# Second layernorm's statistics in two operations instead of three for the later twelve token tiles, with a new order of all operations up to the mix's first tile pair

## The chip, the cores and the metric

The kernel runs on one core of a Trainium2 chip. The metric is device time in microseconds (us) from start to end of one execution, the median of several runs. A core has five engines that each work through their own queue of instructions in order: PE (TensorE, matrix products; PEld is its loading of weights), DVE (VectorE), ACT (ScalarE), POOL (GpSimd) and SP (SyncE, which here only issues DMAs). An instruction waits at the head of its queue until what it reads is there; everything behind it on that engine waits too.

## The reference, cut to what matters

```
x = A_q                                              # [1, 2048, 640], bf16
sa, ca, ga, sb, cb, gb = split((silu(c) @ w_mod), 6)
h = layernorm(x) * (1 + ca) + sa                     # first layernorm
kv = shift_conv(A_k, 4 taps) * A_v                   # short convolution along the tokens
y  = irfft(rfft(kv, 4096) * rfft(ssm_k, 4096))[:2048] + kv * ssm_D   # long convolution
x = x + ga * (h * y)
h = layernorm(x) * (1 + cb) + sb                     # second layernorm: mean and variance over 640 channels
z = gelu(h @ w_in)                                   # 640 -> 1728, tanh form
z1, z2 = z[..., :864], layernorm(z[..., 864:])
g = w_sp @ z2 + b_sp                                 # mix over the 2048 tokens
x = x + gb * ((z1 * g) @ w_out)                      # 864 -> 640
```

## The kernel before, in words

The 2048 tokens are 16 tiles n of 128 (partitions), four groups g of `TB = 4` tiles. The 640 channels are five units u of 128.

The first half works unit by unit. For each unit, PE makes the short convolution with diagonal weights (`dg`); DVE multiplies it with v (L570) and SP transposes the product with DMAs ("kx", L582). The long convolution is a two-step transform. "s1" (stage 1) and its copies to SBUF go first, for the taps ("K") and the signal ("U"). Then come eight steps st: PE's forward ("fwd") of K and U, a copy of the K side by ACT (L247, `KH`), the product by DVE (L463, `Tf`), two sums of its parts by POOL or DVE ("csum", L477, `W`) and PE's inverse ("inv", into `pz`), copied to `Z`. At the end of a unit Z is turned (a DMA, "zt", for units 0 to 3; PE's transposes, "zfl" with copies "zk", for unit 4, whose copies the prediction calls zc), PE makes the last stage y, and DVE multiplies it onto `gh` (L701 "ym", unit 4: L769 "yml"). `gh` holds the first layernorm's output: "ln1" takes its statistics (DVE: L603 and L604; ACT: L599 and L600), "xn" normalizes, and "ghm" (L684, POOL or DVE) multiplies by (1+ca)ga and adds sa ga. "res" (L721) adds `gh` to x (`xt`), and "ln2" (L727) takes the second layernorm's statistics of as many units as are done:

```
            if u not in (1, 3, 4):
                return
            us = range(u - (u < 4), u + 1)
```

So each tile n has three bn_stats: of units 0 and 1 (256 elements), of units 2 and 3 (256), of unit 4 (128). A bn_aggr ("ag2", L852) joins them, then rstd (POOL, L189 and L190, "rstd2"), nmr2 (DVE, L856) and the normalization "zx" (L866 on ACT, L868 on POOL, L870 on DVE). Token group 0 is done in two pieces of two tiles each, so that it gets on sooner; its output is transposed on PE ("hfl", L881) and modulated ("hmod", L892 on ACT, L894 on DVE). Groups 1 to 3 are turned by a DMA ("turn", L912) and modulated by "hmod2".

Then PE makes `zz`, the product with w_in (five matmuls of 432 columns each), ACT the gelu (L943), DVE the statistics of z2 (L949), and DVE or ACT its normalization ("zn", L964). Last is the mix with w_sp over pairs of token tiles (L1036, 48 matmuls of 432 columns for one product group) and the projection with w_out (L1160).

All operations up to the mix's first pair of tiles are not issued where the code stands. Each is recorded in `Plan` with what it reads and writes and with the engines that it may run on; `Plan.run` issues them by `ORDER`, a text written out by hand: a letter for the engine (P, A, D, G for POOL, S) and the number of the operation in the order of recording. So each engine's queue is the letters of its kind, in that order. Waits follow from data and buffers.

Numbers used below, the same in both orders: D36 is the last of the first unit's multiplications with v, S37 and S38 the two DMA transposes of its output, S524 to S527 the loads of the four quarters of x (L589), D532 the ln1 of tile 4, P186 the first forward of unit 0's signal, D187 the first product, P358 the inverse of step 4 of unit 2, G356 and G357 its two sums, G347 a sum of a step before, G446, G447 and G437 sums of unit 3. "gelut" (A133) is a gelu of one small tile that brings ACT's gelu table in. In the order before it stands behind the first gelus. Six "fill" operations are matmuls of the identity (128x512 each; 4, 6, 2, 2, 4 and 3 of them) that nobody reads. In the order before, the fill P1037 (four matmuls) stands between two transposes of unit 4.

Of the kernel before, what the change touches and what calls it, by code (L numbers as in the profile page):

```python
# [31 lines left out]
TB = 4  # L32
# [5 lines left out]


ORDER = """  # L40
A4 A1 S89 D0 G102 P1036 P1035 P7 D13 D15 S2 S90 D14 A16 D101 A10 D103 D116 D117 P1033 S23 G5 D6 A28 A118 D17 D104 D105
P8 A11 D92 A119 D91 A106 D110 D111 A107 P1034 D18 D20 S26 P146 A113 S25 D122 D123 A147 A148 P149 A151 A150 G27 P29 D30
A112 G114 D19 A124 P31 D32 P155 A156 P152 D153 S24 P33 D34 P35 D36 S93 A157 G108 G109 A154 D94 P158 A21 D22 S524 P134
A125 P228 D229 A115 G120 D128 A159 A135 D528 P164 A165 P162 A163 G121 P168 A169 P166 A167 S525 D532 P234 A235 G126
D529 G127 P172 A173 P170 A171 P137 S37 P174 P177 S38 D176 A175 D179 D138 G139 P1038 P140 D141 P183 A178 D184 S39 A530
G41 P180 D181 G42 G136 D531 P230 G54 G142 A182 A185 P186 D187 G188 S40 A231 P202 S52 D203 P232 A533 P43 G189 P45 G53
D44 S3 D46 A233 A534 A535 S527 P196 D197 G198 G199 P248 A249 P47 D48 P49 P190 P9 A12 P160 A161 P212 D50 S51 D536 G537
A191 P200 D213 G214 A543 G215 A201 P222 P55 D223 G224 G225 S566 D56 P218 P204 P192 D219 D193 P59 D538 G554 G555 D60
A544 A129 P252 A253 P206 D207 G131 G132 P143 D144 A205 D556 P236 A237 P254 A255 S526 P57 P194 P258 P242 G145 S95 A545
P250 D58 D259 A243 A251 P567 D539 A568 P569 D540 D541 A195 G67 P256 A257 P61 G550 G551 P220 A546 D96 P260 P302 A221  # L50
A303 P216 G552 D553 S571 G208 G209 D130 D261 P238 A239 P226 A217 A570 P292 P304 P240 A241 D542 D293 P210 P574 P246 D62
G79 A305 D547 S64 A227 D575 G262 G263 A247 P286 D287 A211 P308 A309 P572 P296 G557 D66 D710 D297 G548 D549 P264 P294
A295 D573 P306 A307 P244 P276 P68 A245 S63 P326 D613 D277 D298 P314 P266 A558 D265 P72 D267 A315 A327 P324 A325 G652
D592 G288 G289 P290 A291 P328 A329 G594 P310 A311 S65 D69 A562 P280 D73 D281 G299 P300 P74 D75 P270 A301 P330 A331
P322 S576 P577 A323 G559 G560 A561 P278 A279 D271 D272 D578 D595 D593 P316 D78 P332 A333 G282 G283 D650 A317 D617 S97
S77 D273 P579 D654 D98 P284 P70 D596 D597 P350 D618 A563 A564 D580 G651 S600 P376 A377 A285 D351 P274 A275 P80 D565
G598 D71 G599 P344 D345 G346 G347 P378 P334 A379 D335 G336 G337 D81 P268 A269 P312 A313 P380 A381 P601 D602 P320 A321
P366 D367 P82 P382 A383 D83 P370 D371 P603 P318 D604 S76 D615 P338 A319 G671 P400 A401 G614 P348 A349 D339 P388 A389
P605 P360 P402 A403 P352 A353 G372 D373 D606 P607 G619 G620 D361 G362 P354 D355 P404 A405 P340 D341 P368 D653 P386
A387 D616 P374 A375 P406 D672 A407 P384 A385 P398 S99 G363 A399 P84 D100 D356 G357 D675 P450 A451 D712 D708 G709 A369  # L60
D608 G609 P408 D409 D85 P390 A391 P86 D87 P454 A455 P414 S621 P622 D623 P364 P396 A397 A365 G673 D415 P452 P624 S88
D625 G410 P342 A453 A343 G411 P418 P358 A359 P392 A393 S581 P626 D656 G657 P456 D419 P428 D627 P440 D429 D441 P628
D629 G655 A457 D635 D610 P412 A413 G420 G421 P474 A475 D630 D634 P416 A417 P464 P394 A465 P422 A423 P480 A395 G430
A481 P444 D445 P442 A443 P424 G431 P432 D636 G446 G447 D425 D638 P476 P434 A477 A433 P582 A583 P458 G612 P478 D435
G436 G437 G677 G678 A479 S658 P659 D660 A459 D639 D633 P426 A427 P661 D662 P472 A473 P482 D483 P448 P438 A439 P663
D664 P466 A467 P498 P665 D499 A449 P518 S584 S679 D519 S757 G484 D666 P585 P462 G485 A463 P486 D711 G676 A586 G520
P460 A461 G645 A487 P502 D503 P488 D489 P500 D637 P468 A469 A501 P508 P492 P490 G504 D505 G521 A491 D509 P522 A523
G674 G714 D493 P470 P680 D681 P514 A471 D515 P506 A507 P682 G510 G511 P512 P516 D683 D632 P684 D649 D685 G494 G495
A513 A517 P496 A497 G670 D631 P686 D687 P720 G667 D688 D689 P716 P718 A721 P722 D717 A719 D723 P724 P726 P725 D690
D692 P727 D728 D729 D730 D731 G693 P736 G668 S587 S758 P588 D759 D760 G761 D694 P750 P1037 D732 D733 A589 D691 D762  # L70
A763 P590 A591 D764 D734 D737 D772 D735 D773 P765 D767 D768 D769 D738 G774 D739 P766 A770 A771 D697 G713 D696 D775
A777 D695 D740 D836 P743 P785 A786 D742 D838 P788 A789 P817 A818 D835 G776 P779 D741 D837 A783 D715 D751 D752 P813
D756 A814 G839 D840 D841 A784 P778 D780 D782 P792 A844 D843 G842 A793 P815 A816 D744 P819 S845 A820 P795 A796 D753
D781 P806 D745 D749 P799 A800 A807 D669 D698 D700 G640 G611 D642 P802 A803 D755 D643 P809 D703 A133 S1046 G849 S1045
A846 D644 P823 D747 D707 A810 D704 P825 A826 D702 D904 D706 A848 P821 P827 D641 D701 A822 A828 G847 G850 P851 A852
D748 D699 D790 D746 D901 D903 P858 D902 G905 S1039 D794 P872 D906 D648 A824 D801 D1047 P868 A907 A873 G910 P881 A869
D909 D908 S911 G916 D646 D797 A882 D798 D1054 D1053 D967 A859 P885 A886 D705 P875 P854 D754 S1041 P883 D970 A876 D787
D791 D647 A884 D860 D968 G914 P865 S1040 D870 A855 A866 D867 P861 D969 A862 G971 A915 P889 A890 P891 A892 D1049 A912
P887 A888 P879 D811 A880 D808 D812 D804 D805 G913 P893 D863 D864 A894 D856 D972 D973 D975 G829 P917 A918 D976 D974
S977 D877 D874 D1055 D1056 D830 D833 D831 D853 D871 D857 D878 G895 P927 A928 P941 A942 D943 D1057 D929 P938 A939 D940  # L80
P931 A932 A832 P953 A954 P924 A925 P934 A935 P920 D926 A921 D922 P955 A956 D930 A981 D979 G980 D896 A900 P947 A948
A897 P949 A950 D982 G978 P983 A984 P1000 A1001 P1007 D933 D834 D1052 P1004 A1008 A1005 D1058 D936 P993 A898 A994 P997
A998 D919 D923 D944 D937 G961 D1002 D985 D1009 P986 D1006 D962 D964 D965 D1051 A963 P990 A991 S1042 D999 D1003 D1059
A987 A966 P957 S1043 D1010 P1021 D988 A1022 D989 A958 P1013 A1014 D995 P1015 D992 D996 A899 D1063 D1067 P959 A960
G1027 D1028 D1031 A1016 P945 D1029 A1030 S1044 P1025 A1026 A1032 P1071 A1072 P951 A952 D1064 P1073 D1065 A946 D1066
P1078 A1074 D1068 P1082 D1069 D1070 D1079 D1083 P1075 P1077 D1076 P1084 D1080 S1081 D1085 P1023 A1024 P1017 A1018
P1011 A1012 P1019 D1050 D1048 A1020 D1060 D1061 S1086 D1062
"""


# [39 lines left out]
def kernel(  # L130
# [21 lines left out]
    _, S, D = A_q.shape  # L152
# [28 lines left out]
    st2 = persist.tile([P, NT, 3, SDIM], F32)  # L181
# [13 lines left out]
    mv2 = persist.tile([P, NT, ADIM], F32)  # L195
# [14 lines left out]
    with ExitStack() as pctx:  # L210
# [19 lines left out]
        warm = consta.tile([P, 1], F32)  # L230
# [4 lines left out]
        op = plan.op  # L235
# [478 lines left out]

            return [range(0, 2), range(2, 4)] if g == 0 else [range(g * TB, (g + 1) * TB)]

        def resid(u, g, ns):
            d0 = u * DU
            sl, gl = (x[:, ns[0]:ns[-1] + 1, d0:d0 + DU] for x in (xt, gh))
            k = len(ns) * DU  # L720
            op("GD" if u < NU - 1 else "D", "res", lambda e: e.tensor_tensor(sl, sl, gl, op=ALU.add),  # L721
               r=[("gh", (u, g))], w=[("xt", (u, n)) for n in ns], n=k)
            if u not in (1, 3, 4):
                return
            us = range(u - (u < 4), u + 1)
            for n in ns:
                op("D", "ln2", lambda e, n=n: e.bn_stats(out=st2[:, n, (0, 0, 0, 1, 2)[u], :],  # L727
                                                                          in_=xt[:, n, us[0] * DU:(u + 1) * DU]),
                   r=[("xt", (v, n)) for v in us], w=[("st2", (u, n))], n=len(us) * DU)

# [48 lines left out]
        def small_turn(name, r, fn):  # L779
# [14 lines left out]
           r=["tsk"], w=["sk"])  # L794
# [14 lines left out]
        for i in range(NKC // KCH):  # L809
# [4 lines left out]
           w=["sc"])  # L814
# [34 lines left out]
        get_w_in(0)  # L849
        def norm_piece(g, p, ns, xn2):  # L850
            for n in ns:
                op("D", "ag2", lambda e, n=n: e.bn_aggr(out=mv2[:, n, :], in_=st2[:, n, :, :]),  # L852
                   r=[("st2", (u, n)) for u in (1, 3, 4)], w=[("mv2", n)])
            gs = slice(ns[0], ns[-1] + 1)
            op("G", "rstd2", lambda e: rstd_from_var(rstd2[:, gs], mv2[:, gs, 1]), r=[("mv2", n) for n in ns], w=[("rs2", (g, p))], n=len(ns))
            op("D", "nmr2", lambda e: e.scalar_tensor_tensor(nmr2[:, gs], mv2[:, gs, 0], -1.0, rstd2[:, gs], op0=ALU.mult, op1=ALU.mult),  # L856
               w=[("nm2", (g, p))], r=[("rs2", (g, p))])
            for i, n in enumerate(ns):
                first = i == 0 and p == 0

                def norm(e, n=n, first=first):
# [10 lines left out]
                   w=[(xn2, n % TB)] + ([(xn2, "new")] if first else []), new=[(xn2, "Z")] if first else [])  # L872
# [26 lines left out]
        def z_group(g):  # L899
            ns = range(g * TB, (g + 1) * TB)  # L900
            xn2, hT, z2 = "xn2_%d" % g, "hT%d" % g, "z2_%d" % g
# [24 lines left out]
            for half, lab in ((1, "z2"), (0, "z1")):  # L926
                for i, n in enumerate(ns):
                    for fc in range(NFC):
# [14 lines left out]
                            e.activation(dst, tl[ps][:, :FC], ACT.Gelu_apprx_tanh)  # L943
                        op("P", "zz", mul, r=[(hT, (dt, p_of(n))) for dt in range(ND)] + ["w_in%d" % half],
                           w=[ps] + ([(z2, "new")] if first else []), new=[(ps, tag)] + ([(z2, "X1")] if first else []))
                        op("A", "gelu", gelu, r=[ps] + ([(z2, "new")] if half else []),
                           w=[(z2, (i, fc)) if half else ("z1", (n, fc))])
                        if half:
                            op("D", "stz", lambda e, i=i, n=n, fc=fc: e.bn_stats(out=stz[:, n, fc, :],  # L949
# [284 lines left out]
```

## Time and profile before

| | |
|---|---|
| median of the runs | 308.62 us (308.52, 308.62, 312.23) |
| profiled execution | 307.33 us, of which span 305.5 |
| granted TensorE clock | 1.00 |
| PE busy | 294.8 us (96%), 2,746 matmuls |
| DVE busy | 253.9 us (83%), 529 instructions |
| ACT busy | 162.7 us (53%), 290 |
| POOL busy | 111.0 us (36%), 146 |
| DMA | 42.63 MB, mean 140 GB/s |

The profile covers the span; the profiled execution's own time is 1.83 us longer than it. Busy times are sums over an engine's instructions and say nothing of whether they were on the path that sets the end. For that the busy time by stretch of the span, and for single places the engines' timelines, are read.

### The profile page before, as it was taken

The numbers are of one execution on the slowest core, as the hardware profiler recorded it, in microseconds if no ns is written. First come the engines' busy times: TensorE is split into PE (matmuls) and PEld (weight loads), VectorE is DVE, ScalarE is ACT, GpSimd is POOL, SyncE is SP. The second block draws the span as 40 slices with busy tenths as digits, with TensorE's granted clock in tenths as the row PEclk, the third lists the DMA queues.
The fourth block names the chain that finished last, engine by engine and source line by source line (L and its number), as shares of the span: only waits on it lengthen the run. The fifth ranks groups of instructions, "written<-read, shape, count | busy, mean of one in ns | idle before, by whom it ended". The sixth has DMA issues, their size and how long they took to land.

```text
span 305.5 us, 6890 instructions
## 1 busy us (share of the span) xinstructions
PE 294.8 (96%) x2746; PEld 207.1 (68%) x2746; DVE 253.9 (83%) x529; ACT 162.7 (53%) x290; POOL 111.0 (36%) x146
## 2 busy tenths in 40 slices
PE   7989999999999988989999999999999999999996
PEld 3868998999899878745555555556565656555564
DVE  7999999999999899999869799867675857667474
ACT  6999898998789755586777897030101010010100
POOL 2528778839766889474243311000000000000000
PEclk9999999999999999999999999999999999999999
DMA  8999878995689579007995900092928666540614
GB/s 167 267 180 247 239 190 176 306 202 101 139 88 246 144 144 361 36 3 164 187 175 109 183 2 2 16 181 48 195 66 177 94 148 115 128 103 2 103 30 116
DMA packets 122963, 42.63 MB, mean 140 GB/s; under 512 B 108751, under 2 KB 122932, under 8 KB 122932
## 3 DMA queue, kind: packets, MB, share of 16 engines
q1 hardware_dynamic: 122778, 42.16, 64.8%
q8 instruction: 21, 0.34, 0.5%
q14 instruction: 10, 0.08, 0.1%
q10 hardware_dynamic: 154, 0.05, 0.1%
HBM read 16.11 MB, written 2.62 MB: 61 GB/s over the span
## 4 chain that ended last, share of the span: by engine, by line
PE 80%; DVE 8%; DMA 5%; SPq 3%; ACT 2%; issue 1%; DVEq 0%
PE ps L1036 23%; PE pu L244 18%; PE pz L244 15%; PE po L1160 10%; PE sm L244 7%; PE s L244 3%; DMA ZT<-Z 3%; DMA xt<-in_A_q_dram 3%; PE pz L1036 2%; PE pu L1036 1%; SPq L532 1%; DVE Tf L463 1%; DVE X L247 1%; DVE st L727 1%; DVE gh L701 1%
## 5 line engine op out<-in xcount | busy, mean ns | idle before, releaser
L244 PEld LDWEIGHTS <-Z 128*128 128x128 bf16 x320 | 31.2, 98 | 28.1 <-issue 1.4
L244 PE MATMUL pu<-X,M 128*128 128x128 bf16 (+1 forms) x480 | 45.4, 237 | 3.2 <-DVE X L247 1.5
L1042 ACT COPY m<-ps 128x432 f32<-128x432 f32 x7 | 3.6, 519 | 72.7 <-PE ps L1036 72.7
L244 PEld LDWEIGHTS <-M 128*128 128x128 bf16 x480 | 36.9, 98 | 7.0 <-issue 4.2
L1036 PEld LDWEIGHTS <-S 128*128 128x128 bf16 x256 | 25.0, 98 | 21.7
L477 POOL TENSOR_TENSOR W<-Tf 128x256 bf16<-128x256 f32 x44 | 31.8, 745 | 10.7 <-DVE Tf L463 6.4
L244 PE MATMUL pu<-big,Z 128*128 128x432 bf16 x160 | 32.3, 346 | 1.3 <-ACT X L943 1.3
L247 ACT CAST X<-s 128x1024 bf16<-128x1024 f32 x30 | 30.6, 1019 | 4.2 <-PE s L244 3.7
L1160 PE MATMUL po<-w_o,uT 128*128 128x320 bf16 (+2 forms) x231 | 32.7, 295 | 0.0
L244 PE MATMUL pz<-big,Z 128*128 128x432 bf16 x160 | 32.0, 346 | 0.0
L463 DVE TENSOR_TENSOR Tf<-pu,KH 128x1024 f32<-128x1024 f32 x25 | 30.1, 1216 | 1.6 <-ACT KH L247 0.8
L1036 PEld LDWEIGHTS <-wT 128*128 128x128 bf16 x192 | 18.7, 98 | 15.2
L1160 PEld LDWEIGHTS <-uT 128*128 128x128 bf16 (+1 forms) x231 | 22.2, 98 | 9.7
L247 ACT CAST KH<-pu 128x512 bf16<-128x512 f32 x40 | 23.3, 600 | 6.7 <-PE pu L244 6.4
L244 PEld LDWEIGHTS <-G 128*128 128x128 bf16 x330 | 24.7, 98 | 2.0 <-DVE T L463 0.4
L247 ACT CAST Z<-pz 128x512 bf16<-128x512 f32 x38 | 22.3, 593 | 6.0 <-PE pz L244 5.8
L1036 PE MATMUL ps<-X,wT 128*128 128x432 bf16 x112 | 22.7, 346 | 0.0
L1036 PE MATMUL ps<-T,S 128*128 128x432 bf16 x112 | 22.7, 346 | 0.0
L1036 PE MATMUL ps<-X,S 128*128 128x432 bf16 x112 | 21.6, 346 | 0.0
L949 DVE BATCH_NORM_STATS2 st<-X 128x6 f32<-128x432 bf16 x32 | 18.0, 587 | 4.2 <-ACT X L943 4.2
L244 PE MATMUL sm<-dg,big 128*128 128x128 bf16 x320 | 20.5, 219 | 0.0
L244 PEld LDWEIGHTS <-X 128*128 128x128 bf16 x288 | 17.7, 97 | 2.3 <-DVE X L247 0.4
(190 smaller groups left out, 556.7 us busy)
## 6 DMA issues: line engine op xcount, KB each, us to landing
wm<-in_w_mod_dram SPq DMA_DIRECT2D x6, 800.0 KB, 5.9
xt<-in_A_q_dram SPq DMA_DIRECT2D x4, 640.0 KB, 7.4
out_dram<-ot SPq DMA_DIRECT2D x15, 160.0 KB, 2.1
big<-in_B_w_in_dram SPq DMA_DIRECT2D x2, 1080.0 KB, 5.8
X<-in_A_ssm_k_dram SPq DMA_DIRECT2D x4, 512.0 KB, 8.1
big<-in_A_v_dram SPq DMA_DIRECT2D x2, 1024.0 KB, 6.5
w_o<-in_B_w_out_dram SPq DMA_DIRECT2D x6, 160.0 KB, 3.2
X<-in_A_ssm_k_dram SPq DMA_DIRECT2D x2, 256.0 KB, 3.3
```

The costliest lines, as they stand in the source:

```text
L244: nc.tensor.matmul(o, lhsT=w, rhs=x, start=start, stop=stop)
L247: (e.copy if e is nc.scalar else e.tensor_copy)(dst, src)
L463: e.tensor_tensor(T_[:], (tl[pu] if src is None else tl[src])[:, :, :, None, :].to_broadcast(shape), tl[KH][:, :, None, :, :].to_broadcast ...
L477: e.tensor_tensor(tl[W][:, :, o, :], T_[:, :, 0, o, :], T_[:, :, 1, 1 - o, :], op=ALU.add if o else ALU.subtract)
L532: get(kn, lambda e, h=h: e.dma_start_transpose(tl[kn][:, k0 + h * m:k0 + (h + 1) * m], A_k[0, h * m:(h + 1) * m, dt * P:(dt + 1) * P]), "l ...
L701: op("D", "ym", lambda e: e.tensor_tensor(ghv, ghv, src(), op=ALU.mult), r=[py], w=gk)
L727: op("D", "ln2", lambda e, n=n: e.bn_stats(out=st2[:, n, (0, 0, 0, 1, 2)[u], :], in_=xt[:, n, us[0] * DU:(u + 1) * DU]), r=[("xt", (v, n)) ...
L949: op("D", "stz", lambda e, i=i, n=n, fc=fc: e.bn_stats(out=stz[:, n, fc, :], in_=tl[z2][:, i, fc * FC:(fc + 1) * FC]), r=[(z2, (i, fc))], ...
L1036: nc.tensor.matmul(ps[:, :FC], lhsT=lhs[:, s_, :], rhs=rhs(s_), start=(s_ == 0 and not more), stop=(s_ == HT - 1), skip_group_check=more)
L1042: nc.scalar.copy(part[p, m][:], part[p, BANK[m]][:, :FC])
L1160: nc.tensor.matmul(ps[:, :hi - lo], lhsT=uTs[t][:fsz[ft], ft, :], rhs=w_o[:fsz[ft], ft, lo:hi], start=(ft == 0), stop=(ft == NFT - 1))
```

## The change

There are three parts.

1. For token tiles n of 4 and more (twelve of sixteen), the bn_stats behind unit 3 is dropped, and the one behind unit 4 takes units 2, 3 and 4 at once (384 elements). The bn_aggr joins two groups instead of three. Tiles 0 to 3 stay as they were.
2. Each gelu also reads `warm`, which gelut writes, so that gelut must be issued ahead of the first of them.
3. `ORDER` is new from the first operation to the last. It has twelve operations less (1,075 instead of 1,087), so numbers behind 693 differ between the two orders. Engines are chosen anew as well: to POOL go net three ghm, two res, two xn, two kpad; from DVE go also three zn, two zx and one gcopy to ACT; to DVE come one hmod2, one zc copy and two small ones (a gneg from POOL among them).

```diff
+        LATE = TB
+
         def resid(u, g, ns):
             ...
-            if u not in (1, 3, 4):
+            late = ns[0] >= LATE
+            if u not in ((1, 4) if late else (1, 3, 4)):
                 return
-            us = range(u - (u < 4), u + 1)
+            us = range(u - (2 if late and u == 4 else u < 4), u + 1)
             for n in ns:
-                op("D", "ln2", lambda e, n=n: e.bn_stats(out=st2[:, n, (0, 0, 0, 1, 2)[u], :],
+                op("D", "ln2", lambda e, n=n: e.bn_stats(out=st2[:, n, (0, 0, 0, 1, 1 if late else 2)[u], :],
 ...
-                op("D", "ag2", lambda e, n=n: e.bn_aggr(out=mv2[:, n, :], in_=st2[:, n, :, :]),
-                   r=[("st2", (u, n)) for u in (1, 3, 4)], w=[("mv2", n)])
+                op("D", "ag2", lambda e, n=n: e.bn_aggr(out=mv2[:, n, :], in_=st2[:, n, 0:2 if n >= LATE else 3, :]),
+                   r=[("st2", (u, n)) for u in ((1, 4) if n >= LATE else (1, 3, 4))], w=[("mv2", n)])
 ...
-                        op("A", "gelu", gelu, r=[ps] + ([(z2, "new")] if half else []),
+                        op("A", "gelu", gelu, r=[ps, "warm"] + ([(z2, "new")] if half else []),
```

From the new `ORDER`, the places that the prediction speaks of ("..." where operations are left out):

```diff
-P35 D36 S93 A157 ... P158 A21 D22 S524 ... S525 D532 ... P137 S37 P174 P177 S38 ... S39
+D150 P152 D154 G121 S524 P134 A151 A153 D528 P35 D36 ... S39 ... S93 S37 ... S38 ... S525
-D184 ... P186 A187 ...
+P186 A231 P202 D532 S40 D187 G188 G189 S527
-S526 P57 ...
+A255 P567 S526 D539
-P743 ... P750 P1037 D732 D733 ...
+... P750 ... P1023 G751 ...
-S1086 D1062
+A1008 S1069 A1006 P1025 S1074
```

P1023 is now a fill of two matmuls; P1025, the last PE operation of the list, is the fill of four. G347 to G357 have eight ghm between them on POOL in the new order.

## The prediction

> **What bounds the kernel now.** I read the busy time by stretch first, then the chain that ended last, then the queues of single engines around the places that the change touches. In the stretches the columns are PE, PEld (weight load), DVE, ACT and POOL busy, the granted TensorE clock, the DMA share and GB/s.
>
> ```profile
> 0.00:24.00 24.00, 20.23 (x202) 14.71 (x203) 21.29 (x68) 20.91 (x45) 8.69 (x25) 1.00 1.00 210
> 24.00:95.00 71.00, 70.73 (x982) 65.96 (x981) 68.87 (x118) 62.51 (x108) 54.39 (x64) 1.00 0.87 187
> 95.00:126.00 31.00, 28.58 (x486) 26.03 (x485) 28.88 (x49) 19.38 (x34) 23.74 (x27) 1.00 0.76 205
> 126.00:135.00 9.00, 7.57 (x103) 4.82 (x100) 8.69 (x34) 6.33 (x11) 5.11 (x8) 1.00 0.01 3
> 135.00:200.00 65.00, 65.00 (x362) 34.97 (x360) 57.37 (x145) 44.81 (x81) 19.07 (x24) 1.00 0.52 102
> ```
>
> From 135 us on PE has no gap, so whatever moves the end must move the moment at which the zz matmuls begin to run without a stop (134.16 us here), or add PE work after it. From 24 to 95 PE and DVE are both full (70.7 and 68.9 of 71 us). PE's busy time includes pipelined overlap. Counted in columns instead (five zz matmuls of 432 columns follow each other every 0.912 us, so some 2,400 columns a us), PE has work for about 29.5 of the 40 us between 95 and 135: some 10.5 us are free, and DVE (28.88 of 31, then 8.69 of 9) has almost none. There DVE sets the pace. The head has free PE time too, 8 us up to 31 us.
>
> The end of that stage, in PE's and ACT's timelines (start, duration, what, and in brackets the idle time before it and who ended it):
>
> ```profile
> 126.53 1.02 PE L244 MATMUL s<-ident 128*128 128x512 bf16 x4
> 131.53 1.08 PE L244 MATMUL pu<-big,Z 128*128 128x432 bf16 x5
> 134.16 1.07 PE L244 MATMUL pu<-big,Z 128*128 128x432 bf16 x5 [1.33 <-ACT X L943]
> ```
>
> ```profile
> 131.35 0.92 ACT L866 ACTIVATE Z<-xt,nmr,rstd 128x640 bf16<-128x640 bf16 x1 [1.17 <-DVE nmr L856]
> 132.28 1.28 ACT L943 ACT_TABLE_LOAD   x1
> 133.58 0.53 ACT L943 ACTIVATE X<-pu 128x432 bf16<-128x432 f32 x1
> ```
>
> Three zz operations run, then PE waits for the first gelu, which stands behind a table load of 1.28 us and a normalization of 0.92 us. The line at 126.53 is the fill of four matmuls that nobody reads; it lies in idle PE time.
>
> **The statistics.** Forms of the bn_stats on L727 before:
>
> ```profile
> L727 DVE BATCH_NORM_STATS2 st<-xt x48: 234/408/428, 98.0 to 152.5; 128x6 f32<-128x256 bf16 x32, 128x6 f32<-128x128 bf16 x16
> ```
>
> By form the 128-element ones take 0.273 us and the 256-element ones 0.409. The change removes twelve of 256 (4.9 us) and widens twelve from 128 to 384. No 384 form is in the trace; between the 320-element bn_stats (0.472) and the 432-element one (0.587) I estimate 0.54, bounds 0.47 and 0.59, so +3.2 us. Net about -1.7 us of DVE, bn_aggr hardly changing. But only two of the twelve stand ahead of the first zz in the old order; the other ten run beside continuous PE work, where they cost nothing now and bring nothing. From this part alone: -0.8 us on the path.
>
> **Engine moves ahead of the first zz.** Setting the two lists side by side, DVE's queue ahead of the last hmod (L894) of piece 0 loses: two ln2 0.78; ghm net 1.08; two kpad 0.83; a gcopy 0.68; an xn 0.49; a res 0.45; a zx 0.44; fewer or larger s1 copies 0.53. It gains a csum 0.30, a yml 0.68, a zc copy 0.68 and a gneg. Gneg is not seen on DVE: at least 0.41 (an all-bf16 operation of 512 elements), at most POOL's 1.05; I take 0.68, the DVE copy of the same 1,024 elements. Sum -2.9 us. DVE ends this stage as the fuller engine, so I pass it on: bounds 0 (it only becomes waiting) and -5.3 (half of PE's free 10.5 us, if earlier DVE results also shorten the waits between).
>
> **The head.** SP's and DVE's timelines:
>
> ```profile
> 8.43 1.90 SPq L589 DMA_DIRECT2D xt<-in_A_q_dram x2
> 13.58 3.96 SPq L582 DMA_TRANSPOSE X<-X  x2
> 33.61 0.56 SPq L589 DMA_DIRECT2D xt<-in_A_q_dram x1
> ```
>
> ```profile
> 23.38 0.88 DVE L603 BATCH_NORM_STATS2 st<-xt 128x6 f32<-128x320 bf16 x2
> 24.29 0.21 DVE L604 BATCH_NORM_AGGREGATE mv<-st 128x2 f32<-128x12 f32 x1
> 24.41 1.18 DVE L463 TENSOR_TENSOR Tf<-pu,KH 128x1024 f32<-128x1024 f32 x1
> ```
>
> The transposes of the kv product (S37, S38) wait for D36. The new order puts two more s1 copies (2 x 0.67) and the ln1 of tile 0 (D528, 1.09) ahead of D36 and takes 0.65 away: +1.8 us, S37 at 15.4 instead of 13.58. But D528 reads x's first quarter, S524. With S93 now behind it that load is issued at about 7.8 and, by the 6.9 to 8.0 us that the four loads of L589 took to land, is there at 15.2 at the median of 7.4. So D528 ends at 16.3, D36 at 16.9, and S37 goes then. The second quarter (S525), issued at 9.80 before, now stands behind both transposes, which hold SP for 3.96: 20.9, landed at 27.8 with the 6.9 that S526 took on a like queue. Its first reader, the ln1 of tile 4 (D532), stands in DVE's queue directly ahead of D187, the first product; every product, sum and inverse of unit 0 is behind it. D187 begins at 27.8 + 1.1 = 28.9, not 24.41: 4.5 late. About 1.0 of DVE work that came later before has been done by then, so DVE loses 3.5 us: **+3.5** (0 if S37 goes at 15.4 and the load lands in some 4 us; 4.6 with the slowest landing). The third quarter (S526) now follows the second kv transpose, whose input is about 2 us later: lands at about 42.5, its reader ran at 41.42 when it landed at 40.53: **+0.5** (0 to 1.5).
>
> **POOL.** Net three ghm, two res and two xn go to POOL, at very different prices:
>
> ```profile
> L684 DVE TENSOR_TENSOR gh<-gh,gca_bf x12: 409/414/917, 51.9 to 91.1; 128x512 bf16<-128x512 bf16 x12
> L684 POOL TENSOR_TENSOR gh<-gh,gsa_bf x11: 1151/1156/1357, 67.8 to 130.1; 128x512 bf16<-128x512 bf16 x11
> L684 DVE TENSOR_TENSOR gh<-gh,gsa_bf x9: 361/419/948, 64.0 to 133.0; 128x512 bf16<-128x512 bf16 x9
> ```
>
> POOL's work ahead of its first rstd2 grows from 88.4 to 95.1 us by these rows. It has room on average, but not everywhere. Between two sums of unit 2, G347 and G357, the new list puts eight ghm (9.2 us) and the csums, 16.0 us together, where DVE has 12 to 13 and PE about 14.4. Before, POOL waited for others in this stretch:
>
> ```profile
> 80.81 1.41 POOL L477 TENSOR_TENSOR W<-Tf 128x256 bf16<-128x256 f32 x2 [0.79 <-DVE Tf L463]
> 83.24 1.01 POOL L477 TENSOR_TENSOR W<-Tf 128x256 bf16<-128x256 f32 x1 [1.01 <-PE pz L244]
> 86.04 1.16 POOL L684 TENSOR_TENSOR gh<-gh,gsa_bf 128x512 bf16<-128x512 bf16 x1 [1.79 <-DVE gh L684]
> ```
>
> Behind G357 waits the inverse P358, on PE behind it the next forwards, and behind those DVE's products. The excess is 1.6 us against PE and 3.5 (16.0 less 12.5) against DVE, less what POOL has in hand when the stretch begins; it may be all of it. Bounds 0 and 3.5; I take **+0.9**, half of the excess against PE and a little. The Trainium skill ("Perfetto Trace Analysis", Optimizing Scalar/DVE Operations) warns that GpSimd and VectorE share an SBUF read port, so that moving work between them may not help. The rows show the cost of that only at the extremes: 0.95 at most against a DVE median of 0.42. By the page the relief of the ghm moves would be nothing, and the sum about 1.1 higher.
>
> **The tail.** Let X be the end of the second bn_aggr of piece 0 (126.01 before). In the new list nmr2 comes at X + 1.75 (before X + 1.2), two yml stand ahead of the hmods, the gelu table is loaded in unit 4's stage (the gelut operation now stands ahead of every gelu), and the zx of tiles 2 and 3 both go to ACT, 0.92 each, one after the other. Following these durations, zz runs without a stop from X + 8.95; before, X + 8.15. The table load spares 1.28 in the gelu, but 0.93 of that is spent on the second zx, and 0.8 goes to the later nmr2 and the yml: **+0.5** (bounds -1.3, the whole table load, and +1.5). The Trainium skill ("ScalarE: Activation LUTs", What ACT_TABLE_LOAD costs) gives about 1.28 us for the load and 1.38 more for a drain. Here the gelu starts 1.30 us after the load does, so no drain is seen; by the page the sum would be 1.4 lower. The next token group's turn is issued at X + 12.45 instead of X + 11.5; its last hmod2 ended at 145.96, with 0.4 us to spare: **+0.5** (0 to 1.5).
>
> **The last fill.** The fill of four (126.53 above) is now PE's last operation of the list, directly ahead of the mix's pair 1, where PE is the bound: 4 x 512 columns, 0.213 us each, **+0.85**. A fill of two takes its place at 126.5 and costs nothing while PE idles there.
>
> **Sum.** -2.9 + 3.5 + 0.5 + 0.9 + 0.5 + 0.5 + 0.85 = +3.85 us. The profiled execution took 307.33 (span 305.5, 1.83 around it), so 311.2; the median of the runs lies 1.29 above the profiled one, so 312.5.
>
> **Rivals.**
> Rival 1, DVE's relief goes through in full: between 95 and 135 half of PE's free time is recovered (-5.3), the table load too (-1.3), and the head's delay disappears in PE's 8 free us there, the fill in some stall: 308.6 - 6.6 = 302.0. For it: DVE 93 to 97% full there. Against: PE has only 0.27 us without work from 24 to 95, and ten of twelve removed statistics are after the first zz.
> Rival 2, POOL becomes the bound: G357 late by the full 3.5, again 2.0 at unit 3's sums (G446, G447, G437), and the five operations of the ghm and res moves each stretch a DVE neighbour from 0.42 to 0.95 (+2.65). With the other terms (+2.95): 308.6 + 2.95 + 8.15 = 319.7. It decides once G357 ends over 2 us after PE has come to P358. For it: 1.16 on POOL against 0.42 on DVE; against: POOL has 16.6 of 71 us free.
> Rival 3, the change does nothing where it matters: two of twelve statistics count, and the order is a wash: 308.6, within 1 us.
>
> **How the numbers follow.** Forecast 0.46, rival 1 0.14, rival 2 0.28, rival 3 0.12. A measurement of this kernel tells about 2% from no change: 302.4 and 314.8. Faster by over 2%: 0.10 of rival 1. Slower by over 2%: 0.24 of rival 2 and 0.12 of the forecast, whose terms pass +6 when two or three of them are at their upper bounds. The rest, 0.54, is within 2%. The likeliest case's own range is 307 to 317; the 8-in-10 range reaches to the rivals, 303 to 319.5.
>
> **What would show it.** Right: D187 at about 29 us with the wait on xt's DMA ahead of it; POOL without idle time between 70 and 95 and PE waiting at P358 for W on L477; no ACT_TABLE_LOAD near the first gelu; a fill of four directly ahead of the mix; zz without a stop from 136 to 138; L727 forms of 384 elements near 0.54. Wrong: a first product before 25.5 (head), DVE idle of several us between 95 and 126 (relief not passed on), or zz without a stop from before 131 (rival 1) or after 141 (rival 2).

## The result, and the profile after

The changed kernel takes 311.76 us (median; 311.12 to 312.34) beside 308.57 for the kernel before: a ratio of 1.0128, 95% interval 1.0096 to 1.0160. It is slower by 1.3%, clearly, but by less than 2%. The ratio is formed from the undisturbed executions alone, so it is not the quotient of the two medians. The profiled execution took 311.21 us, with a span of 309.1 (307.33 and 305.5 before). The time was forecast within 0.8 us. But the forecast got there with two large errors of opposite sign, and the cause is one that it had only in a rival.

The same stretches of the span as before, with the same columns (PE, PEld, DVE, ACT, POOL busy, granted clock, DMA share, GB/s):

```profile
0.00:24.00 24.00, 20.57 (x198) 14.86 (x199) 21.60 (x71) 19.64 (x40) 10.56 (x26) 1.00 0.92 210
24.00:95.00 71.00, 68.36 (x936) 63.23 (x934) 67.52 (x102) 62.12 (x111) 57.66 (x68) 1.00 0.90 192
95.00:126.00 31.00, 29.55 (x472) 27.13 (x469) 29.38 (x43) 23.10 (x39) 25.53 (x28) 1.00 0.75 194
126.00:135.00 9.00, 8.55 (x146) 6.16 (x147) 8.56 (x28) 2.84 (x6) 6.02 (x9) 0.81 0.01 2
135.00:200.00 65.00, 64.38 (x360) 34.54 (x359) 57.26 (x144) 44.06 (x80) 19.24 (x25) 1.00 0.49 97
```

Between 24 and 126 us DVE executes 145 instructions instead of 167, and is busy nearly as long: 96.9 us instead of 97.75. Nothing in this table says why. The lines of single groups do. These are the residual additions and the modulation by line, engine and form, with the minimum, median and maximum duration in ns:

```profile
L722 DVE TENSOR_TENSOR xt<-xt,gh x10: 292/416/1358, 83.0 to 143.9; 128x512 bf16<-128x512 bf16 x8, 128x256 bf16<-128x256 bf16 x2
L683 DVE TENSOR_TENSOR gh<-gh,gca_bf x10: 412/417/1375, 50.5 to 98.1; 128x512 bf16<-128x512 bf16 x10
L683 DVE TENSOR_TENSOR gh<-gh,gsa_bf x8: 415/467/1196, 67.0 to 99.5; 128x512 bf16<-128x512 bf16 x8
```

The same residual line before:

```profile
L721 DVE TENSOR_TENSOR xt<-xt,gh x12: 291/416/426, 96.8 to 141.0; 128x512 bf16<-128x512 bf16 x10, 128x256 bf16<-128x256 bf16 x2
```

It had a maximum of 426 ns. Now the same operation takes up to 1,358, the ghm up to 1,375. Two of these operations, each with what POOL does meanwhile (start, duration, engine, line):

```profile
91.01 1.20 DVE L683 TENSOR_TENSOR gh<-gh,gsa_bf 128x512 bf16<-128x512 bf16 x1
92.13 1.21 DVE L462 TENSOR_TENSOR Tf<-pu,KH 128x1024 f32<-128x1024 f32 x1
```

```profile
90.76 1.17 POOL L722 TENSOR_TENSOR xt<-xt,gh 128x512 bf16<-128x512 bf16 x1
```

```profile
54.59 2.05 DVE L683 TENSOR_TENSOR gh<-gh,gca_bf 128x512 bf16<-128x512 bf16 x3
56.56 1.21 DVE L462 TENSOR_TENSOR Tf<-pu,KH 128x1024 f32<-128x1024 f32 x1
```

```profile
55.19 1.17 POOL L683 TENSOR_TENSOR gh<-gh,gca_bf 128x512 bf16<-128x512 bf16 x1
```

The first ends at 92.21, the POOL operation at 91.93. The last of the three ends at 56.64, the POOL operation at 56.36. Both times DVE ends 0.28 us after POOL: it looks as if it had stood still until POOL was through, and then did its 0.3 us. This is no accident of two places. Three ghm or residuals of 512 elements took over 0.5 us before, seven after, and ten in the run b_dummy below. All twenty began beside a POOL operation that was already running, and ended 0.28 us after it. The products on L462 stand directly behind in DVE's queue and are late by as much.

Counted up to DVE's last hmod of piece 0, DVE's operations go from 202 to 195, its busy time (each operation from the end of the one before it) from 123.19 to 125.62 us, its idle time from 6.75 to 7.57. So the hmod (the last of three in one line, first before, then after) ends at 133.19 instead of 129.94:

```profile
128.96 0.98 DVE L894 TENSOR_SCALAR Z<-s,cb_col,sb_col 128x256 bf16<-128x256 bf16 x3
```

```profile
132.14 1.04 DVE L896 TENSOR_SCALAR Z<-s,cb_col,sb_col 128x256 bf16<-128x256 bf16 x3
```

By kind, ghm takes 0.94 us more although there are two fewer of them, res 1.19 more with one fewer, nmr1 0.70 more, the product of a tap block with D 0.62 more. (nmr1 is a small operation of the first layernorm, on 8 elements.)

The first zz that runs without a stop, and the end of the list, in PE's timeline; the last line is the begin of the mix before:

```profile
137.04 1.08 PE L243 MATMUL pu<-big,Z 128*128 128x432 bf16 x5
202.01 1.08 PE L243 MATMUL pz<-big,Z 128*128 128x432 bf16 x5
202.93 1.03 PE L243 MATMUL s<-ident 128*128 128x512 bf16 x4
204.01 1.25 PE L1038 MATMUL ps<-X,wT 128*128 128x432 bf16 x6
```

```profile
200.38 1.62 PE L1036 MATMUL ps<-X,wT 128*128 128x432 bf16 x8
```

zz runs without a stop from 137.04 (134.16 before), the mix begins at 204.01 (200.38): 2.9 us come from ahead of zz, and 0.7 more from there to the mix, where the fill now stands. From the mix on both take 105.1 us.

### The profile page after: what moved, and what is told of

Its sections match the earlier page's. It is cut to its first block, busy times and chain, and to the rows that moved or that the text cites. A ratio compares the mean times of both kernels' runs of the same rounds, so it can differ in the third digit from the quotient of the medians.

```text
span 309.1 us, 6884 instructions
## 1 busy us (share of the span) xinstructions
PE 297.6 (96%) x2746; PEld 208.3 (67%) x2746; DVE 255.7 (83%) x509; ACT 161.9 (52%) x290; POOL 119.0 (38%) x154
## 4 chain that ended last, share of the span: by engine, by line
PE 78%; DVE 7%; DMA 6%; SPq 4%; ACT 4%; issue 1%; POOL 0%; DVEq 0%
PE ps L1038 23%; PE pu L243 16%; PE pz L243 14%; PE po L1162 10%; PE sm L243 7%; PE s L243 4%; SPq L531 3%; DMA wm<-in_w_mod_dram 2%; DMA X<-X 2%; PE pz L1038 2%; DMA X<-in_A_ssm_k_dram 2%; DVE Tf L462 1%; ACT X L246 1%; PE pu L1038 1%; DVE T L462 1%
## 5 line engine op out<-in xcount | busy, mean ns | idle before, releaser
L476 POOL TENSOR_TENSOR W<-Tf 128x256 bf16<-128x256 f32 x44 | 32.5, 759 | 15.4 <-DVE Tf L462 11.9
L246 ACT CAST X<-s 128x1024 bf16<-128x1024 f32 x31 | 31.7, 1022 | 6.1 <-PE s L243 6.0
L462 DVE TENSOR_TENSOR Tf<-pu,KH 128x1024 f32<-128x1024 f32 x25 | 30.1, 1215 | 0.7 <-POOL W L476 0.4
L246 ACT CAST Z<-pz 128x512 bf16<-128x512 f32 x37 | 21.5, 593 | 4.0 <-PE pz L243 3.6
```

What stands on the lines that cost most here:

```text
L246: (e.copy if e is nc.scalar else e.tensor_copy)(dst, src)
L462: e.tensor_tensor(T_[:], (tl[pu] if src is None else tl[src])[:, :, :, None, :].to_broadcast(shape), tl[KH][:, :, None, :, :].to_broadcast ...
L476: e.tensor_tensor(tl[W][:, :, o, :], T_[:, :, 0, o, :], T_[:, :, 1, 1 - o, :], op=ALU.add if o else ALU.subtract)
```

## The experiments

In the labels, a_ is made from the changed kernel and b_ from the kernel before. All ratios are to the kernel before, measured anew beside each set of runs, with medians of 307.25 (a_fill, a_kx1, a_ghm, a_all), 307.77 (b_stats, b_gelut, b_eng, a_eng) and 307.71 us (the others).

### First theory: gaps on PE and the last fill

The first reading of the two traces counted PE's time without work, in columns as in the prediction. After had 1.7 us more of it at 38 us (a first stage of unit 1 that waited for its DMA transpose), 1.5 more between 46 and 65 (products late behind four early ghm), and the fill of four at the end. Theory A took these as the loss.

a_fill moves the last fill up:

```diff
-... A1006 P1025 S1074
+... P588 A589 P1023 P1025 G751 A752 ...
```

> The changed kernel with one operation moved: the fill of four matmuls goes from the end of PE's list to directly behind the fill of two, ahead of the first zz, where PE has idle time. Theory A (the fill at the end stands on the path in full): 0.85 us less than the changed kernel, so a ratio to before near 1.010 instead of 1.0128. Rival: the first mix product waits for something else there (a weight, a sum of tiles), and the fill is hidden: no change, 1.0128.

Measured: 311.25 us, 1.0132 (1.0104 to 1.0160): no gain. The trace shows that the new place has no idle time to give:

```profile
130.56 2.50 PE L243 MATMUL s<-ident 128*128 128x512 bf16 x6
132.90 0.95 PE L243 MATMUL sm<-Ebd,X 128*128 128x16 bf16 x32
133.70 0.49 PE L883 MATMUL s<-ident,Z 128*128 128x128 bf16 x6
```

The transposes L883 come directly behind and are pushed back. The run shows that PE was not free there; it says nothing yet about the end of the list. a_fill1, later, cut the fill itself:

```diff
-FILLS = (4, 6, 2, 2, 4, 3, )
+FILLS = (4, 6, 2, 2, 1, 3, )
```

> The changed kernel with the last fill of one matmul instead of four (left out: three matmuls that nobody reads). The prediction's step: PE is the bound there, 3 x 0.213 = 0.64 us less, ratio near 1.011. Rival: the mix's first product waits for a weight or a sum of tiles there, and PE idles instead, 1.0128.

Measured: 310.98 us, 1.0102 (1.0069 to 1.0135). That is where the prediction's step would have it, but the interval also holds 1.0128. The trace decides for the step: from the fill's begin to the mix's begin 0.44 us pass with one matmul, 1.08 with four. So the fill is on the path there, with 0.64 us for three matmuls.

a_kx1 fills PE's gap at 37.37:

```diff
-... S51 P252 D253 ... P57 P216 ...
+... S51 P57 P252 D253 ... P216 ...
```

> The changed kernel with one PE operation moved: the taps P57 go directly ahead of the first s1 of unit 1 (P252), which waited 1.29 us for the DMA transpose of its input. Theory A (PE sets the pace from 31 to 95 us, so a gap there is never made up): about 1.0 us of the gap is filled and comes through at the end, ratio near 1.009. Rival B (the stretch from 95 to 137 us is paced by DVE and by chains between engines, and absorbs early gaps): 0 to 0.3 us, ratio 1.012 to 1.013.

Measured: 311.28 us, 1.0139 (1.0118 to 1.0161): no gain. The wait of 1.29 us shrinks to 0.27, and the next s1 waits instead:

```profile
37.27 0.61 PE L243 MATMUL s<-F1bdU,X 128*128 128x256 bf16 x4 [0.27 <-DMA X<-X]
37.72 0.60 PE L243 MATMUL pz<-W,G 128*128 128x256 bf16 x6
39.20 0.60 PE L243 MATMUL s<-F1bdU,X 128*128 128x256 bf16 x4 [0.88 <-DVE X L246]
```

The gap has moved by 1.5 us. PE's order was not what was short: the second s1 waits for DVE's copy of the first half, that copy for the first s1, and this one for the DMA transpose, and begins at 37.27 instead of 37.37. So the gap was moved and not filled, and the run doesn't say what the late transpose costs.

a_ghm moves the four ghm later in DVE's list (594 ahead of 595, 650 ahead of 651, 615 and 696 to 80.6 and 84.3 us):

```diff
-... D287 D594 ... D615 D650 ... D696 ... D297 ...
+... D287 ... D297 ... D594 D595 ... D650 D651 ... D361 D615 ... D87 D696 ...
```

> The changed kernel with four DVE operations moved later in DVE's list: the ghm D594, D615, D650 and D708 (the numbers of the changed order: 594, 615, 650, 696), which stood ahead of the product D297 at 54.3 to 56.6 us, go to where they are first needed or to about 80 us. Theory A: the three PE waits on Tf at 54.40, 57.83 and 60.03 (1.03 us together) and the slow growth of PE's idle time beside them go, 1.0 to 1.5 us less at the end, ratio 1.008 to 1.0095. Rival B: the same DVE work is only moved to a place where DVE is as full, the waits appear there, ratio 1.012 to 1.014.

Measured: 313.37 us, 1.0202 (1.0183 to 1.0221): slower. PE is busy 9.96 of 10 us between 55 and 65 (9.12 in the changed kernel), and only 22.46 of 25 between 65 and 90 (24.69):

```profile
55.00:65.00 10.00, 9.96 (x134) 9.20 (x133) 9.45 (x12) 8.76 (x12) 9.13 (x12) 1.00 1.20 246
65.00:90.00 25.00, 22.46 (x312) 20.63 (x310) 24.80 (x37) 18.98 (x31) 21.02 (x22) 1.00 0.71 151
```

The gap went where the work went, and grew. DVE is what is full, not one place of its list.

a_all had all three moves.

> The three moves together in the changed kernel: the fill, the taps P57 and the four ghm. Theory A: the gains add up, 0.85 + 1.0 + 1.2 = 3.0 us less than the changed kernel, a ratio near 1.003. Rival B: only the fill's 0.85, ratio near 1.010.

Measured: 314.04 us, 1.0214 (1.0193 to 1.0235). So theory A has fallen as far as it was tried: moving work into or out of its three places gives nothing back, and only the length of the fill was shown to count.

### What the parts are worth alone

b_stats is the kernel before with the change of the statistics alone:

```diff
-            if u not in (1, 3, 4):
+            late = ns[0] >= LATE
+            if u not in ((1, 4) if late else (1, 3, 4)):
 ...
-... D694 ... D695 ...   (the twelve ln2 behind unit 3 of tiles 4 to 15)
+...                     (four of the wide ones behind the residual they read)
```

> The kernel before with the change of the statistics alone: its own sequence and engines, the twelve bn_stats behind unit 3 dropped, the twelve behind unit 4 over 384 elements (four of these moved a few places later in DVE's list, behind the residual that they now read). The prediction's step: two of the twelve stood ahead of the first zz, so 0 to 0.8 us faster, ratio 0.997 to 1.000. Rival: the wider operations stand in the tail where DVE paces the next token groups (piece 1 and group 1), up to 1 us slower, 1.000 to 1.003.

Measured: 307.56 us, 1.0013 (0.9986 to 1.0040). The statistics are worth nothing that can be measured, as expected from where they stand.

b_gelut is the kernel before with gelut moved:

```diff
-... A513 A517 ...      ... P809 D703 A133 S1046 ...
+... A513 A133 A517 ... ... P809 D703 S1046 ...
```

> The kernel before with one ACT operation moved: gelut goes from behind the first gelus to about 119 us, so the table load of 1.28 us leaves the tail (it stood ahead of the first gelu at 132.28). The prediction's step: the first gelu starts up to 1.3 us earlier, PE's stop of 1.33 us goes, 0.8 to 1.3 us faster, ratio 0.996 to 0.9975. Rival: the load at about 119 us delays the zc copies on ACT, and the last of them is what unit 4's transposes wait for: no change or 1 us slower, 1.000 to 1.003.

Measured: 306.77 us beside 307.77, 0.9979 (0.9959 to 0.9998). By its ratio this is the fastest version of the study. The load now stands between two copies:

```profile
118.88 1.28 ACT L815 ACT_TABLE_LOAD   x1
120.17 0.20 ACT L815 ACTIVATE warm<-warm 128x1 f32<-128x1 f32 x1
```

PE's stop of 1.33 us in the zz is gone; the fourth zz begins at 132.91 instead of 134.16:

```profile
132.91 1.07 PE L244 MATMUL pu<-big,Z 128*128 128x432 bf16 x5
```

So this part of the change is a true gain, 1.2 us at this place of the trace and 0.6 us in the ratio, and the loss elsewhere is larger than the total shows.

b_eng and a_eng split the new order in two: the old sequence with the new engines, and the new sequence with the old engines. Only letters of the order change.

```diff
-... G594 ... D654 ...      (b_eng, two of many: each letter as in the changed order;
+... D594 ... G654 ...       a_eng has the new sequence with the letters of before)
```

> The kernel before, its own sequence of operations and its three statistics per tile, but every operation on the engine that the changed order gives it (POOL gets net three ghm, two res, two xn, two kpad more; DVE the rest of the trade). Theory C (DVE sets the pace up to the first zz, and its operations that read two bf16 tensors from SBUF take up to 1.3 us instead of 0.34 while POOL works beside them): the 2.9 us that DVE gives away by rows come back as stretching, 0 to 3 us slower, ratio 1.00 to 1.01. Rival (the prediction's own step: what leaves DVE is gained, and the loss is in the sequence): 2 to 3 us faster, ratio 0.990 to 0.994.

> The changed kernel's sequence and statistics, but every operation on the engine that it had before. Theory C: POOL has 6 to 7 us less beside DVE, the stretched ghm, res and nmr fall back towards 0.35 us; DVE has 2.9 us more by rows and 3 to 5 us less stretching, so 0 to 2 us faster than the changed kernel, ratio 1.006 to 1.013. Rival (the loss is in the sequence and DVE's relief was real): 2 to 3 us slower than the changed kernel, ratio 1.019 to 1.023.

Measured: 339.74 us, 1.1069 (1.1021 to 1.1117), and 348.11 us, 1.1305 (1.1273 to 1.1338). Both theories had said within 2.5%, and both are wrong by far. Each hybrid leaves DVE idle: 29.8 us up to the last hmod in b_eng and 20.4 in a_eng, beside 6.75 and 7.57. A list fits only the engines that it was written for. Which single swaps cost the most was not followed up, so these two runs say nothing on the question that they were made for.

### Theory C: DVE is stretched by POOL

Three runs test the reading of the profile after. a_less leaves POOL operations out, so that DVE's neighbours are gone and DVE's own list is the same:

```diff
-            o["fn"](engines[e])
+            if i not in SKIP:
+                o["fn"](engines[e])
+SKIP = (673, 698, 620, 614, 609, 645)
```

> The changed kernel without six operations of POOL between 51 and 103 us (four ghm and two res, old numbers 673, 710, 620, 614, 609 and 645; so these products, sums and residuals are left out). Each of them or its neighbour ran beside a DVE operation that took 0.5 to 1.0 us too long (ln1f, ghm 708, res 611, ghm 616, res 630). Theory C (DVE sets the pace and is stretched by POOL): DVE's last hmod of piece 0 comes 2.5 to 3.5 us earlier, 2 to 3 us less in all, ratio 1.003 to 1.007. Rival (POOL is off the path, the loss is in waits between PE, SP and DVE): at most 0.5 us, ratio 1.011 to 1.014.

Measured: 309.65 us, 1.0064 (1.0044 to 1.0084): 2.0 us less than the changed kernel. DVE's busy time up to the last hmod falls from 125.62 to 122.97 us, with the same operations, and the hmod ends at 131.56 instead of 133.19, 1.6 us earlier where 2.5 to 3.5 were expected. Its idle time grows by 1.0 us, so the gain is not from shorter waits: shorter are ln1f (the end of the first layernorm's statistics, 1.35 us), ghm (0.84) and res (0.43). Six ghm and residuals still last over 0.5 us. The longest residual on DVE (here L726) takes 930 ns instead of 1,358:

```profile
L726 DVE TENSOR_TENSOR xt<-xt,gh x10: 292/420/930, 81.9 to 142.3; 128x512 bf16<-128x512 bf16 x8, 128x256 bf16<-128x256 bf16 x2
```

b_less is the control:

```diff
+SKIP = (673, 652, 620, 614, 609, 645)
```

> The control: the kernel before without six operations of POOL of the same kinds between 54 and 112 us (673, 652, 620, 614, 609, 645; left out likewise). In the old order only one of them runs beside a stretched DVE operation. Theory C: 0 to 0.6 us less, ratio 0.998 to 1.000. Rival (less work on POOL as such makes either kernel faster, for POOL's sums come sooner): 2 us or more, ratio 0.994 or below.

Measured: 307.36 us, 0.9996 (0.9973 to 1.0020). The same amount of POOL work less, and nothing gained: DVE's busy time is 97.64 us between 24 and 126 (97.75 before). Five of the six operations are the very same ones as in a_less. So in the old order neither POOL's load nor its lateness costs anything that was measured; together with a_less, what counts is which DVE operation POOL meets.

b_dummy adds POOL operations that nobody waits for:

```diff
+EXTRA = {651: 6, 709: 3, 446: 5}
 ...
+            for _ in range(EXTRA.get(i, 0)):
+                self.extra()     # tensor_tensor(xtra, xtra, xtra) on POOL, 128x224 bf16
             o["fn"](engines[e])
```

> The kernel before with fourteen additional POOL operations (bf16 additions of 224 elements on a tile that nobody reads, about 0.5 us each), put into gaps in which POOL waits: six ahead of G651 (gap of 4.85 us up to 67.82), three ahead of G709 (1.79 us up to 86.04), five ahead of G446 (3.0 us up to 99.70). In these gaps DVE runs ghm, kpad and res. They fit the gaps, so no POOL result is late. Theory C: DVE's ghm at 84.9 and res at 96.8 take 0.3 to 0.6 us longer each, 1 to 2.5 us slower, ratio 1.003 to 1.008. Rival: nobody waits for these operations, ratio 1.000.

Measured: 310.66 us, 1.0089 (1.0057 to 1.0122): 2.7 us slower, a little over theory C's range. The additions took 0.7 us each, not 0.5. The gap ahead of G446, POOL first and DVE second:

```profile
99.45 3.30 POOL L781 TENSOR_TENSOR xtra<-xtra 128x224 bf16<-128x224 bf16 x5
103.36 1.42 POOL L482 TENSOR_TENSOR W<-Tf 128x256 bf16<-128x256 f32 x2 [0.61 <-DVE Tf L468]
```

```profile
99.67 2.02 DVE L726 TENSOR_TENSOR xt<-xt,gh 128x512 bf16<-128x512 bf16 x3
101.73 0.43 DVE L732 BATCH_NORM_STATS2 st<-xt 128x6 f32<-128x256 bf16 x1
```

Three residuals take 2.02 us; in the kernel before they took 1.10 (at 96.84). The bn_stats next to them takes 0.43, as ever. POOL's next real operation still waits 0.61 us for DVE's product, and behind the other two groups 2.31 and 0.70 us for DVE, so POOL is not late: the additions cost only what they take from DVE. DVE's busy time up to the last hmod grows by 4.2 us, and the hmod ends at 133.20, 3.3 later, the same as in the changed kernel. Nothing but the meeting of the two engines has cost the old order 2.7 us, beside the 3.9 (by the ratio) of the changed kernel.

## Why the prediction was right, and where it was wrong

**DVE's relief, -2.9: wrong, the step that failed.** The net count of operations was right (202 to 195), with two slips that cancel: of the net three ghm one stood behind the last hmod in the old list already, and no csum is gained (six in both). The rows of before gave each its price. But these rows were themselves taken from an order in which DVE's two-tensor operations seldom met POOL: there three of 20 ghm and none of six residuals up to this hmod took over 0.5 us, in the new order five of 18 and two of five. The busy time rose by 2.4 us: the term was wrong by 5.3 us, and with the other sign. Rival 2 had priced the same stretching at 2.65 for five operations and tied it to a POOL that comes late; a_less and b_dummy show that it needs no late POOL. The Trainium skill ("Perfetto Trace Analysis", Optimizing Scalar/DVE Operations) says that the two engines share an SBUF read port, so that moving work between them might not help. The prediction had quoted this and given it 1.1 us. The runs agree with the page and show more: it can cost more than it brings. Two readings of the lists ahead of the prediction are to be put right, neither on this path: net three zn go from ACT to DVE, not the other way, and stand behind the first zz; and what the prediction calls a zc copy is a copy of an inverse into Z, not one of unit 4's transposes.

**The head, +3.5: wrong, and it hid the other error.** D187 began at 24.36, against 24.41 before; the prediction had named a first product before 25.5 as the sign that this term is wrong.

```profile
15.31 3.02 SPq L581 DMA_TRANSPOSE X<-X  x2
```

```profile
23.17 0.88 DVE L602 BATCH_NORM_STATS2 st<-xt 128x6 f32<-128x320 bf16 x2
24.36 1.22 DVE L462 TENSOR_TENSOR Tf<-pu,KH 128x1024 f32<-128x1024 f32 x1
```

The transposes went at 15.31, where the plain count of DVE's queue had them (15.4). The load of x's first quarter, issued at 7.70, was there for a bn_stats at 13.61: under 5.9 us. The second was issued at 18.37 and read at 23.17: under 4.8. The prediction had taken the 6.9 to 8.0 us of the loads before for a property of the load. They were also not four times but two: the trace before has a landing for only two of the loads. In the trace after, the four took 4.5 to 9.2 us. What makes the difference is not shown; the DMA share was about 1.0 from 5 to 24 us in both traces. The prediction's own lower bound (a landing after some 4 us) was right.

**x's third quarter, +0.5:** its reader ran at 42.02 instead of 41.42, with no idle time of DVE directly ahead of it. What is late in this place is the transposed kv product of unit 1. PE's first stage waited 1.29 us for it, and DVE 1.16 for PE:

```profile
37.37 0.61 PE L243 MATMUL s<-F1bdU,X 128*128 128x256 bf16 x4 [1.29 <-DMA X<-X]
```

```profile
38.02 1.23 DVE L246 CAST X<-s 128x1024 bf16<-128x1024 f32 x1 [1.16 <-PE s L243]
```

This is DVE's longest idle time ahead of the last hmod, and more than the 0.82 us by which its idle time grows there in all. So this lateness belongs to the 3.25 us of the hmod by the same account as the stretching. The prediction had the late input but priced only the load behind it. No run took it away (a_kx1 left 1.18 us of it), so what it costs at the end stays open.

**POOL, +0.9: wrong, it cost nothing in this way.** POOL was without a gap from 75 to 85 us as foreseen, but none of PE's waits of 0.15 us or more from 30 us to zz is for a sum of POOL (L476). DVE waited for one twice, 0.15 us at 43.29 and 0.24 at 111.31, neither in the stretch that was feared.

**The tail, +0.5:** from the second bn_aggr of piece 0 (128.72) zz runs without a stop after 8.32 us; before, 8.15. So +0.2. Inside it the table load brought a gain, as b_gelut shows. The rule of the Trainium skill ("ScalarE: Activation LUTs", What ACT_TABLE_LOAD costs), 1.28 us and a drain of 1.38, is again seen with the first part alone: in b_gelut the activation starts at 120.17, 1.29 after the load does, and the stop that went was 1.33.

**The turn, +0.5:** nothing. From 140 to 200 us PE begins the same 328 matmuls, with as many columns, in both kernels.

**The last fill, +0.85:** right. 1.08 us pass from its begin to the mix's, 0.44 with one matmul instead of four.

**The statistics:** right that they don't matter. Widened bn_stats took 0.56 alone and 1.42 for three in a row; 0.54 was estimated. b_stats puts their whole worth within 0.4% of nothing.

So the sum of +3.85 met +3.2 in the median (+3.9 by the ratio and between the profiled executions) by luck: the head was overestimated by 3.5, POOL, the turn and the third quarter had terms of 1.9 together that were not seen in that form, and DVE was underestimated by 5.3. The mechanism ahead of zz that holds is: DVE is the pace up to the last hmod, where its own work got 2.4 us longer and its waits 0.8. Of the 3.6 us in the span, the six POOL operations of a_less account for 2.0 (by the ratios; 1.2 between the profiled executions) and the fill for 0.7 to 0.9; the rest, with b_gelut's gain against it, is not told apart. The stretching left in a_less and the wait at 38.02 would be the first to look at.

## What to carry to other kernels

A duration read from a trace holds for the neighbours that the operation had there; before a sum of rows is believed, look at the maximum beside the median, and at what the other engine did in the instances that were long. When work moves from VectorE to GpSimd in a kernel where VectorE sets the pace, count for every operation of VectorE that reads two tensors from SBUF whether a GpSimd operation will run beside it, for that can cost more than the move saves. And a hand-written order and its choice of engines are one thing: swapping either alone cost over 10% here, so they are tried together or not at all.

## What the runs showed of the hardware

- DVE operations with two SBUF inputs in bf16 (512 elements, 0.41 us alone, 0.34 from one to the next) could last 0.5 to 1.4 us when a POOL operation was running as they began. All twenty over 0.5 us in the traces before, after and b_dummy ended 0.28 us after that operation. That they stand still until then is an inference from these times. DVE operations with PSUM input (the products, 1.17 to 1.23 us; the y products of 512 elements, 0.63 to 0.69) and bn_stats (0.44 to 0.50 for 320 elements) took the same with and without POOL beside them.
- It is not two tensors alone: xn and zx on DVE, a tensor_scalar of 640 bf16 elements, took 0.44 us alone and, in four instances beside POOL in the traces before and after, 0.56 to 1.10.
- Small ones suffer too: nmr1 on 8 elements took 0.32 and 0.69 us beside POOL's sums and 0.16 without.
- POOL's own durations hardly changed: its median for 512 elements is 1.15 us in both kernels.
- A DMA's time to landing differed by a factor of two for loads of the same size (640 KB) in one program: 4.5 to 9.2 us from issue in the kernel after, 6.9 and 8.0 before.
- In the profiled execution after, the granted clock was 0.81 between 126 and 135 us. Another execution of the same kernel with a mean clock of 1.000 had the same span of 309.1, so it is not part of the loss.
